# Reordering the first loads, transposes and cluster assignments of a routed-attention kernel, with one weight load and two lerps moved

## The chip, the cores and the metric

One core of one Trainium2 chip. The metric is device time in microseconds (us) of one execution. A few executions came out some per cent slower than the rest of the same kernel; they are called slow. All runs quoted as times are fast ones unless a sentence says otherwise. The time before was 252.65 us as the median of four executions (252.64 to 252.88; the three made first gave 252.67).

## The reference, cut to what matters

4 batches, 8 heads, 768 positions, 64 columns a head. Every query and key is assigned to the nearest of its head's 16 centroids; a query sees only the keys of its own cluster. The output goes through a channel mix with three matrix products.

```python
c_n = centroids / (np.linalg.norm(centroids, axis=-1, keepdims=True) + 1e-06)   # 8 x 16 x 64
q_assign = np.argmax(np.einsum('bhsd,hcd->bhsc', q_n, c_n), axis=-1)            # k_assign alike
mask = q_assign[:, :, :, None] == k_assign[:, :, None, :]
scores = scale * np.matmul(q, k.transpose(0, 1, 3, 2))
scores = np.where(mask, scores, -1000000000.0)
attn = softmax(scores) @ v                                   # shortened here
# x: the heads side by side, 4 x 768 x 512; x_prev: x one position earlier
xk = mu_k * x + (1.0 - mu_k) * x_prev
xr = mu_r * x + (1.0 - mu_r) * x_prev
k = np.maximum(xk @ w_k, 0.0)
v = k * k @ w_v
r = 1.0 / (1.0 + np.exp(-(xr @ w_r)))
return r * v
```

## The kernel before

The kernel walks through 192 score steps: 16 pairs of heads, 12 steps a pair. One step is a score product on TensorE (PE), an exponential on ScalarE (ACT) and, six steps later, the product with the values. The mask costs no pass of its own: each operand of the score product has 64 rows of data and 16 rows with the one-hot of its cluster.

```python
def scores(t):
    ...
    nc.tensor.matmul(st[:, 0:512], kc, a[rows, 0:512], start=True, stop=True)      # L286
    nc.tensor.matmul(st[:, 512:S], kc, a[rows, 512:S], start=True, stop=True)      # L287
    nc.scalar.activation(pt, st, AF.Exp, bias=-BIG, scale=BIG)                     # L289
```

The one-hot rows come in two ways. Pair 0 is done at the start in pieces: transposes of q and k (`first_trans`), products with the centroids (`first_aff`), one-hots transposed back and copied, half by VectorE (DVE) and half by ACT (`first_onehot`). From pair 1 on, one product `affps` is followed on DVE by a transpose, a maximum, a comparison and a transpose, and a DMA on SyncE's queue (SP) puts the rows `oht` into `aug`.

The order at the start, which the change alters, with cuts:

```python
nc.scalar.dma_start(cn_sb, centroids.rearrange("h c d -> (h c) d"))   # 32 KB
nc.scalar.preload_act_table(AF.Sqrt)
load_head(0, nc.sync, nc.scalar)          # q of pair 0 on SP's queue, k on ACT's, 192 KB each
...
use_pe(8)                                 # warm-up products on zeros
...                                       # norms of the centroids on DVE and ACT
nc.tensor.transpose(cnt_ps.rearrange("d h c -> d (h c)"), cn_sb, ident)
nc.vector.tensor_copy(cblk[0:64, :, 0, :], cnt_ps)
nc.vector.tensor_copy(cblk[64:128, :, 1, :], cnt_ps)
first_trans(0, 0)
first_trans(0, 1)
use_pe(4)
first_trans(1, 0)
first_aff(0, 0)
first_aff(0, 1)
first_trans(1, 1)
first_aff(1, 0)
...
first_onehot(0)
first_aff(1, 1)
```

What is put beside the steps. `forced` runs on PE within a step, `at` behind it:

```python
for i in range(4):
    at(7 + i // 2, load_wk, i)            # four pieces of w_k, GpSimd's queue
forced = {
    0: lambda: more(1, 0, 4, nc.vector, ps_o),    # transposes of pair 1
    1: lambda: more(1, 4, 4, nc.vector, ps_o),
    2: lambda: more(1, 8, 4, nc.vector, ps_o),
    3: lambda: first_onehot(1),
    4: lambda: aff_mm(1),
}
...
at((62, 66, 70, 74)[n] if n < NP else x + 4, sh2)   # the lerp into xr on DVE, L358
```

From step 58 on, slices of the channel mix (`psk`, `psr`, `psv`) are pushed in between. `psr` needs `xr`.

The softmax here doesn't subtract the row's maximum and nothing guards it: scores larger than these inputs give would overflow.

Of the kernel before, what the change touches and what calls it, by code (L numbers as in the profile page):

```python
# [16 lines left out]
def kernel(  # L17
# [13 lines left out]
    nc = tc.nc  # L31
# [4 lines left out]
    NP = H // 2  # L36
# [32 lines left out]
    ps_o = ctx.enter_context(tc.tile_pool(name="ps_o", bufs=2, space=bass.MemoryType.PSUM))  # L69
# [21 lines left out]
    def load_head(h, eng_q, eng_k):  # L91
        if h == 0:
            nat[0] = loadp.tile([128, 2, 2 * GW], F32, name="qk_rows", tag="qk_nat")
        for i, (src, eng) in enumerate(((q, eng_q), (k, eng_k))):
            eng.dma_start(
                nat[0][:, i, h * GW:(h + 1) * GW].rearrange("p (m e) -> p m e", e=2 * D),
                src[0, h].rearrange("(m p r) d -> p m (r d)", p=128, r=2))
# [128 lines left out]
    def first_trans(t, i):  # L226
        if t == 0 and i == 0:
            qkT[0] = qktp.tile([128, 4, GW], F32, name="qkT")
        g = 2 * i + t
        ps = ps_w.tile([128, GW], F32, name="trps0", tag="w") if t == 0 else \  # L230
            ps_o.tile([128, GW], F32, name="trps1", tag="out2")
        for c2 in range(NCH // 2):
            m = t * GW + c2 * 128
            nc.tensor.matmul(ps[:, c2 * 128:(c2 + 1) * 128], nat[0][:, i, m:m + 128], ident,
                             is_transpose=True, start=(c2 == 0), stop=(c2 == NCH // 2 - 1))
        if i == 0:
            nc.vector.tensor_copy(qkT[0][:, g, :], ps)
        else:
            nc.scalar.copy(qkT[0][:, g, :], ps)
        casts(0, g)  # L240

    def first_aff(t, i):
        if i == 0:
            first[t] = ps_w.tile([128, 2, NCH, C], F32, name="aff0", tag="w") if t == 0 else \
                ps_o.tile([128, 2, NCH, C], F32, name="aff1", tag="out2")
        ps = first[t]
        for c2 in range(NCH // 2):
            nc.tensor.matmul(ps[:, i, 2 * c2:2 * c2 + 2, :], qkT[0][:, 2 * i + t, c2 * 128:(c2 + 1) * 128],
                             cblk[:, t, :, :], start=True, stop=True)
        if i == 1:  # L250
            rmax = clup.tile([128, 2 * NCH], F32, name="rmax0")
            psv = ps.rearrange("p i c e -> p (i c) e")
            nc.vector.tensor_reduce(rmax, psv, axis=AX.X, op=ALU.max)
            oh = first[t] = clup.tile([128, 2 * NCH, C], BF16, name="oh0")
            nc.vector.tensor_tensor(oh, psv, rmax[:, :, None].to_broadcast([128, 2 * NCH, C]),
                                    op=ALU.is_ge)
# [187 lines left out]
    def at(t, fn, *args):  # L444
        todo.setdefault(t, []).append(lambda: fn(*args))

    with tc.manual_schedule():

        warm = constp.tile([128, 512], BF16)
        nc.vector.memset(warm, 0.0)  # L450
        nc.scalar.dma_start(cn_sb, centroids.rearrange("h c d -> (h c) d"))
        nc.scalar.preload_act_table(AF.Sqrt)
        load_head(0, nc.sync, nc.scalar)
        load_head(1, nc.sync, nc.scalar)
        load_rows(1, nc.sync, nc.scalar)
        load_v(0, nc.sync)
# [3 lines left out]
        def use_pe(m):  # L460
            wps = ps_st.tile([128, S], F32, name="wps", tag="st")
            for i in range(m):
                nc.tensor.matmul(wps[:, 0:512], warm[:, 0:128], warm, start=True, stop=True)  # L463
# [13 lines left out]
        cn_rnorm = constp.tile([H * C, 1], F32)  # L477
        nc.vector.reciprocal(cn_rnorm, cn_norm)
        nc.vector.tensor_scalar_mul(cn_sb, in0=cn_sb, scalar1=cn_rnorm)
        cnt_ps = ps_o.tile([D, H, C], F32, name="cnt_ps", tag="out2")  # L480
        nc.tensor.transpose(cnt_ps.rearrange("d h c -> d (h c)"), cn_sb, ident)
        nc.vector.tensor_copy(cblk[0:64, :, 0, :], cnt_ps)
        nc.vector.tensor_copy(cblk[64:128, :, 1, :], cnt_ps)
        first_trans(0, 0)
        first_trans(0, 1)
        use_pe(4)
        first_trans(1, 0)
        first_aff(0, 0)
        first_aff(0, 1)
        first_trans(1, 1)  # L490
        first_aff(1, 0)
        load_rows(2, nc.sync, nc.sync)
        load_v(1, nc.sync)
        vcast(0)
        for i in range(1, NX):
            init_ring(i)
        first_onehot(0)
        first_aff(1, 1)

        def more(n, i, m, eng=None, pool=None):  # L500
            for i in range(i, i + m):
                trans_pe(n, i, eng or nc.vector, pool)
# [24 lines left out]
        at(6, load_mu)  # L527
        at(31, less_one)
        for i in range(4):
            at(7 + i // 2, load_wk, i)  # L530
            at((29, 53, 55, 57)[i], load_wv, 2 * i)
            at((60, 62, 64, 66)[i], scale_wv, 2 * i)
        for i in range(2):
# [2 lines left out]
        W = 2 * NCH  # L536

        forced = {
            0: lambda: more(1, 0, 4, nc.vector, ps_o),
            1: lambda: more(1, 4, 4, nc.vector, ps_o),  # L540
            2: lambda: more(1, 8, 4, nc.vector, ps_o),
            3: lambda: first_onehot(1),
            4: lambda: aff_mm(1),
        }
        at(3, load_rows, 3, nc.sync, nc.sync)
# [2 lines left out]
        for n in range(NPAIR):  # L548
            s = n * W
            off = (6, 3, 2, 1)[n] if n < NP else 0  # L550
            if n + 4 < NPAIR:
                if n + 4 < NP + 2:
                    at(s + (16 if n == 0 else 9), load_rows, n + 4, nc.sync, nc.sync)
                elif n < NP:
                    for i in range(8):
                        at(s + (8 if n == 2 else 12) + i // 2, load_qk, n + 4, i // 4, i % 4)
                else:
                    for i in range(8):
                        at(s + (12 if n == NP else 9) + i, load_qk, n + 4, i // 4, i % 4)
            if n + 2 < NPAIR:  # L560
                if n < NP:
                    for i in range(6):
                        forced[s + i + off] = lambda n=n, i=i: more(n + 2, 2 * i, 2)
                    a = (13, 10, 9, 8)[n]
                    h = 1 if n == 0 else 2
                    for i in range(h):
                        forced[s + a + i] = lambda n=n, i=i, h=h: aff_mm(n + 2, i, h)
                    d = a + h - 5
                else:
                    if n == NP:  # L570
                        a = (9, 10, 11, 12, 15)
                    elif n == NP + 1:
                        a = (3, 4, 5, 6, 11)
                    elif n == NP + 2:
                        a = (1, 2, 3, 4, 9)
                    elif n == NP + 3:
                        a = (0, 1, 2, 3, 8)
                    else:
                        a = (-1, 0, 1, 2, 5)
                    for g in range(4):  # L580
                        at(s + a[g], trans, n + 2, g)
                    forced[s + a[4]] = lambda n=n: aff_mm(n + 2)
                    d = a[4] - 4
                at(s + 5 + d, aff_max, n + 2)
                at(s + 6 + d, aff_back, n + 2, [nc.sync])
                at(s + (3 if n == 0 else 8), load_v, n + 2, nc.sync)
            if n + 1 < NPAIR:
                at(s + 7, vcast, n + 1)
            at(s + W - 1, norm, 2 * n)
            e = s + W + NCH  # L590
            at(e - 1, norm, 2 * n + 1)
            if n == 0:
                at(e + 3, xtr, n)
            elif n < NP - 1:
                for i in range(3):
                    at(e + 3 + i, xtr, n, i, 3)
            elif n in (NP - 1, NPAIR - 1):
                x = e + (3 if n < NP else 2)
                at(x - 1, xtr, n)
            else:  # L600
                at(e, xt_dma, n)
                x = e + (4 if n % NP == NP - 1 else 6 if n == NPAIR - 2 else 14)

            def sh(n=n):
                b, j = divmod(n, NP)
                if j == 0:
                    mixes[b] = Mix(b)
                mixes[b].shift(n)

            def sh2(n=n):  # L610
                b, j = divmod(n, NP)
                mixes[b].shift_r(n)

            def enq(n=n):
                b = n // NP
                queue.extend(mixes[b].slices())
                rate[0] = len(queue) / (H * NCH + (b == 0)) if b < B - 2 else (len(queue) - HOLD) / (H * NCH - NCH - 4)
                credit[0] = 0.0
            at((33, 48, 50)[n] if n < NP - 1 else x, sh)
            at((62, 66, 70, 74)[n] if n < NP else x + 4, sh2)  # L620
            if n % NP == NP - 1:
                at(e + 4 if n < NP else x + 1, enq)

# [49 lines left out]
```

## Time and profile before

| | before |
|---|---|
| median, us | 252.65 |
| span of the profiled execution, us | 250.9 |
| PE busy / idle, us | 238.7 / 12.2 |
| first score (step 0) starts | 10.87 |
| step 5, the first score after the affinities of pair 1 | 15.57 |
| step 24, the first score of pair 2 | 32.33 |
| step 72, the first score of pair 6 | 75.01 |
| step 84 | 89.91 |
| last score (step 191) starts | 210.04 |

The prediction below shows the profile's lines themselves. From the timeline at the start of the kernel before (start, length, engine, line, operation, output<-input, in brackets the idle time before it and what ended that):

```profile
3.10 0.22 DVE L470 CUSTOM_DVE_ANT_0 cn_sq<-cn_sb 128x64 f32<-128x64 f32 x1 [1.70 <-DMA cn_sb<-in_centroids_dram]
...
11.39 3.11 ACT L289 ACTIVATE pt<-st 128x768 bf16<-128x768 f32 x4 [0.67 <-PE st L287]
```

The centroids are first used at 3.10 us. The first four exponentials take 3.11 us together: they run back to back.

### The profile page before, as it was taken

What the parts mean: (1) busy time and instruction counts of PE and PEld (TensorE: products, weight loads), DVE (VectorE), ACT (ScalarE), POOL (GpSimd) and SP (SyncE); (2) the same over time, 40 slices, a digit from 0 to 9 for tenths busy, and PEclk for the clock granted to TensorE, in tenths of its full rate; (3) what the DMA queues carried; (4) which work ended last, traced back from release to release, by engine and by line L of the source; (5) the groups of instructions that cost most, each with busy time, mean ns of one, the idle gap of its engine ahead of it and who ended that gap; (6) DMA issues with size and microseconds to landing.
All of it is one profiled execution on the core that took longest, in us unless ns stands there. A gap on an engine that the chain in (4) does not pass through costs nothing.

```text
span 250.9 us, 6203 instructions
## 1 busy us (share of the span) xinstructions
PE 238.7 (95%) x2364; PEld 146.5 (58%) x2395; DVE 176.6 (70%) x340; ACT 189.4 (75%) x271; POOL 106.0 (42%) x190
## 2 busy tenths in 40 slices
PE   8999989998998999999999999999999998899994
PEld 3866766765665555555676555556566555355442
DVE  3576778698899994979967778679844427865222
ACT  5398988999897977878999877878899785146210
POOL 2968848571999737080827153712801000000000
PEclk9999999999999999999999999999999999999999
DMA  6995897879978586965959689794121121110122
GB/s 176 260 258 94 153 280 143 112 140 168 178 114 170 92 176 127 201 123 120 206 67 157 80 185 131 167 163 152 34 79 29 47 70 48 56 72 0 70 98 86
DMA packets 102462, 31.87 MB, mean 127 GB/s; under 512 B 74721, under 2 KB 98977, under 8 KB 102433
## 3 DMA queue, kind: packets, MB, share of 16 engines
q1 hardware_dynamic: 98352, 27.97, 54.3%
q0 software_dynamic: 2208, 2.62, 7.0%
q10 hardware_dynamic: 1872, 0.89, 1.3%
q8 instruction: 19, 0.31, 0.5%
q14 instruction: 11, 0.08, 0.1%
HBM read 24.15 MB, written 6.29 MB: 121 GB/s over the span
## 4 chain that ended last, share of the span: by engine, by line
PE 75%; DVE 10%; ACT 8%; issue 2%; DMA 2%; SPq 0%; DVEq 0%; ACTq 0%
PE psv L405 15%; PE st L286 13%; PE out L299 10%; PE psk L382 10%; PE psr L394 7%; ACT pt L289 7%; PE st L287 6%; PE psk L373 5%; PE affps L194 4%; DMA aug<-oht 2%; PE wps L463 2%; DVE xr L358 2%; DVE k L388 1%; DVE oht L217 1%; DVE xk L358 1%
## 5 line engine op out<-in xcount | busy, mean ns | idle before, releaser
L289 ACT ACTIVATE pt<-st 128x768 bf16<-128x768 f32 x192 | 148.2, 811 | 23.2 <-PE st L287 22.8
L175 POOL TENSOR_SCALAR aug<-qkT 64x384 bf16<-64x384 f32 x128 | 74.8, 584 | 73.1 <-DVE qkT L145 52.2
L286 PE MATMUL st<-aug 80*128 80x512 bf16 x192 | 73.1, 381 | 2.5 <-ACT pt L289 1.0
L299 PEld LDWEIGHTS <-pt 128*128 128x128 bf16 x1152 | 59.9, 97 | 26.6 <-ACT pt L289 1.4
L299 PE MATMUL out<-vt,pt 128*128 128x65 bf16 x1152 | 66.0, 193 | 0.9 <-ACT pt L289 0.8
L287 PE MATMUL st<-aug 80*128 80x256 bf16 x192 | 51.9, 270 | 0.0
L405 PE MATMUL psv<-w_v_sb,k 128*128 128x512 bf16 x173 | 44.5, 378 | 1.4 <-ACT tanh L397 0.7
L387 ACT ACTIVATE kr<-psk 128x512 bf16<-128x512 f32 x48 | 28.8, 601 | 8.1 <-PE psk L382 5.6
L388 DVE TENSOR_TENSOR k<-kr 128x512 bf16<-128x512 bf16 x48 | 22.4, 473 | 17.0 <-ACT kr L387 16.9
L382 PE MATMUL psk<-xk,w_k_sb 128*128 128x512 bf16 x113 | 30.6, 378 | 1.5 <-DVE t L198 0.8
L412 DVE SCALAR_TENSOR_TENSOR out_sb<-tanh,psv 128x512 f32<-128x512 bf16 x23 | 15.7, 682 | 21.7 <-PE psv L405 17.8
L286 PEld LDWEIGHTS <-aug 80*128 80x128 bf16 x192 | 18.7, 97 | 17.3 <-issue 7.8
L397 ACT ACTIVATE tanh<-psr 128x512 bf16<-128x512 f32 x24 | 14.4, 599 | 19.1 <-PE psr L394 18.5
L405 PEld LDWEIGHTS <-k 128*128 128x128 bf16 x184 | 16.1, 97 | 16.4 <-issue 2.4
L287 PEld LDWEIGHTS <-aug 80*128 80x128 bf16 x192 | 18.9, 98 | 9.7 <-issue 1.6
L394 PE MATMUL psr<-w_r_sb,xr 128*128 128x512 bf16 x91 | 23.7, 378 | 0.2
L145 DVE STREAM_TRANSPOSE qkT<-qk_nat 128x384 f32<-128x384 f32 x40 | 21.5, 557 | 0.0
L182 POOL CAST vt<-v_nat 128x384 bf16<-128x384 f32 x32 | 17.0, 560 | 9.5 <-DMA v_nat<-in_v_dram 8.7
L312 DVE TENSOR_TENSOR xn<-out,rs 128x384 bf16<-128x384 f32 x32 | 17.8, 558 | 1.1
L198 DVE STREAM_TRANSPOSE t<-affps 128x384 f32<-128x384 f32 x15 | 8.7, 580 | 14.0 <-PE affps L194 13.9
L382 PEld LDWEIGHTS <-w_k_sb 128*128 128x128 bf16 x128 | 11.2, 97 | 10.2 <-issue 0.9
L358 DVE SCALAR_TENSOR_TENSOR xk<-diff,mu_k_sb,xt 128x768 bf16<-128x768 bf16 x16 | 16.7, 1043 | 0.6
(65 smaller groups left out, 206.2 us busy)
## 6 DMA issues: line engine op xcount, KB each, us to landing
v_nat<-in_v_dram SPq DMA_DIRECT2D x16, 384.0 KB, 4.2
out_dram<-out_sb SPq DMA_DIRECT2D x23, 256.0 KB, 2.8
qk_nat<-in_q_dram SPq DMA_DIRECT2D x40, 96.0 KB, 4.3
qk_nat<-in_k_dram SPq DMA_DIRECT2D x40, 96.0 KB, 3.6
qk_rows<-in_q_dram SPq DMA_DIRECT2D x5, 384.0 KB, 4.4
qk_rows<-in_k_dram SPq DMA_DIRECT2D x4, 384.0 KB, 5.3
aug<-oht SPq DMA_DIRECT2D x60, 24.0 KB, 2.0
w_k_sb<-in_moe_w_k_dram POOLq DMA_DIRECT2D x4, 256.0 KB, 5.6
```

Source lines behind the costliest of these rows:

```text
L145: nc.vector.transpose(qkT[n][:, g, :], nat[n][:, g // 2, (g % 2) * GW:(g % 2 + 1) * GW])
L175: nc.gpsimd.tensor_scalar(augv(n, g)[0:64, par, :], in0=qkT[n][64 * par:64 * par + 64, g, :], scalar1=qk_scale, scalar2=1.0, op0=ALU.mult, ...
L286: nc.tensor.matmul(st[:, 0:512], kc, a[rows, 0:512], start=True, stop=True)
L287: nc.tensor.matmul(st[:, 512:S], kc, a[rows, 512:S], start=True, stop=True)
L289: nc.scalar.activation(pt, st, AF.Exp, bias=-BIG, scale=BIG)
L299: nc.tensor.matmul(o[:, (qc + NCH // 2) % NCH, :], pts[bh * NCH + c][:, qc * 128:(qc + 1) * 128], vts[n % NR][:, tt, 2 * (c % 3) + c // 3, ...
L358: nc.vector.scalar_tensor_tensor(out=d, in0=diff, scalar=mu[:, j:j + 1], in1=cur, op0=ALU.mult, op1=ALU.add)
L382: nc.tensor.matmul(ps, w_k_sb[:, j, ii * 128:(ii + 1) * 128], self.xk[:, j, 0:512], start=(j == 0), stop=(j == NJ - 1))
L387: nc.scalar.activation(kr, src, AF.Relu)
L388: nc.vector.tensor_tensor(dst, kr, kr, op=ALU.mult)
L394: nc.tensor.matmul(ps, self.xr[:, j, sl], w_r_sb[:, j, :], start=(j == 0), stop=(j == NJ - 1))
L405: nc.tensor.matmul(self.psvt, self.k2[:, i, sl], w_v_sb[:, i, :], start=(i == 0), stop=(i == NI - 1))
```

## The change

The intent: q and k of the first heads, the large loads, should not stand behind the small one; PE should transpose them instead of waiting for the centroids; and head 1's clusters, wanted only at step 6, should not delay head 0's first score. One w_k load moves out of the way of the cluster rows of pair 2, and two lerps move behind an affinity transpose that PE awaits. I name the five parts A to E.

```diff
+        load_head(0, nc.sync, nc.scalar)                                    # A
         nc.scalar.dma_start(cn_sb, centroids.rearrange("h c d -> (h c) d"))
         nc.scalar.preload_act_table(AF.Sqrt)
-        load_head(0, nc.sync, nc.scalar)
 ...
+        first_trans(0, 0)                                                   # B
+        first_trans(0, 1)
         cnt_ps = ps_o.tile([D, H, C], F32, name="cnt_ps", tag="out2")
 ...
-        first_trans(0, 0)
-        first_trans(0, 1)
         use_pe(4)
-        first_trans(1, 0)                                                   # C
         first_aff(0, 0)
         first_aff(0, 1)
+        first_trans(1, 0)
         first_trans(1, 1)
-        first_aff(1, 0)
 ...
         first_onehot(0)
-        first_aff(1, 1)
+        first_aff(1, 0)
 ...
-            at(7 + i // 2, load_wk, i)
+            at((7, 7, 8, 27)[i], load_wk, i)                                # D
 ...
-            0: lambda: more(1, 0, 4, nc.vector, ps_o),
-            1: lambda: more(1, 4, 4, nc.vector, ps_o),
-            2: lambda: more(1, 8, 4, nc.vector, ps_o),
-            3: lambda: first_onehot(1),
+            0: lambda: first_aff(1, 1),                                     # C
+            1: lambda: more(1, 0, 4, nc.vector, ps_o),
+            2: lambda: more(1, 4, 4, nc.vector, ps_o),
+            3: lambda: (more(1, 8, 4, nc.vector, ps_o), first_onehot(1)),
 ...
-            at((62, 66, 70, 74)[n] if n < NP else x + 4, sh2)
+            at((62, 66, 72, 75)[n] if n < NP else x + 4, sh2)               # E
```

## The prediction

> **What bounds the kernel now.** I read the page first. One core, span 250.9 us, TensorE at full granted clock and busy 95%:
>
> ```profile
> span 250.9 us, 6203 instructions
> ...
> PE 238.7 (95%) x2364; PEld 146.5 (58%) x2395; DVE 176.6 (70%) x340; ACT 189.4 (75%) x271; POOL 106.0 (42%) x190
> ```
>
> So all idle time of PE is 250.9 - 238.7 = 12.2 us, and a change of order alone, with the same work, can only win or lose there. The table of stretches says where that idle time is (columns: stretch, its length, then busy us of each engine, clock, DMA share, GB/s):
>
> ```profile
> 0.00:11.00 11.00, 9.62 (x62) 6.69 (x63) 4.57 (x15) 4.52 (x6) 5.81 (x19) 1.00 0.74 203
> 11.00:21.50 10.50, 9.86 (x105) 6.75 (x104) 7.81 (x13) 9.94 (x13) 7.73 (x20) 1.00 0.77 210
> 21.50:33.00 11.50, 10.77 (x147) 7.37 (x148) 8.16 (x17) 9.26 (x13) 10.29 (x21) 1.00 0.84 161
> 33.00:50.00 17.00, 16.48 (x230) 12.04 (x228) 12.88 (x25) 16.04 (x22) 10.14 (x19) 1.00 0.91 174
> ...
> 70.00:79.00 9.00, 8.10 (x81) 4.95 (x82) 8.93 (x16) 7.26 (x12) 8.25 (x11) 1.00 0.75 126
> ...
> 90.00:215.00 125.00, 122.49 (x1248) 73.86 (x1269) 90.77 (x178) 102.76 (x148) 42.54 (x72) 1.00 0.61 116
> ```
>
> Three regimes. Until about 60 us the exponentials pace the kernel (9.94 of 10.50 us of ACT busy in the second line, 16.04 of 17.00 in the fourth). From 70 to 79 us DVE is full, 8.93 of 9.00, and PE loses 0.90. After 90 us PE is full. A delay or gain of the ramp that survives to 60 us is carried to the end one for one, because from there a fixed amount of PE work follows. Busy PE in the first 11 us proves nothing: 12 of its matmuls are warm-ups on zeros.
>
> Next the chain of waits, in order of time (start, length, what), for the point that limits the ramp:
>
> ```profile
> 25.55 0.99 DVE oht L217
> ...
> 26.56 0.51 SPq L219
> 27.07 0.04 issue
> 27.12 5.12 DMA aug<-oht
> 32.24 0.09 issue
> 32.33 0.38 PE st L286
> ```
>
> Step 24, the first scores of pair 2, waits for the 24 KB cluster rows, 5.12 us under way. The waits of PE give that stop as 0.7 us, and the later one as 0.8 us:
>
> ```profile
> PE st L286 <- DMA aug<-oht: 0.7, 1, 0.7
> ```
>
> ```profile
> PE psk L382 <- DVE t L198: 0.8, 1, 0.8
> ```
>
> Last the timeline at the start, which the change reorders:
>
> ```profile
> 3.59 1.28 ACT L475 ACT_TABLE_LOAD   x1
> ...
> 3.99 0.25 DVE L479 TENSOR_SCALAR cn_sb<-cn_sb,cn_rnorm 128x64 f32<-128x64 f32 x1
> ...
> 4.79 0.94 PE L234 MATMUL trps<-ident,qk_rows 128*128 128x128 f32 x6
> 5.04 0.28 DVE L482 COPY cblk<-cnt_ps 64x128 f32<-64x128 f32 x1 [0.79 <-PE cnt_ps L481]
> ...
> 6.76 1.42 PE L248 MATMUL aff<-cblk,qkT 128*128 128x32 f32 x12
> ...
> 9.94 0.79 ACT L271 COPY aug<-ohps 16x768 bf16<-16x768 bf16 x1 [0.88 <-PE ohps L264]
> ```
>
> Centroids are ready at 4.24, affinities run from 6.76 to 8.18, the one-hots end with ACT's copy at 10.73, the first score starts at 10.87.
>
> **What the Trainium skill says.** (1) DMA: Bandwidth & Descriptors, "Queues, rings and completion order": each SDMA engine round-robins between the queue rows that have work, packet by packet, and takes the descriptors of one ring in order. The trace agrees: the pair-1 cluster rows issued at 18.90 landed in 1.9 us; the same 24 KB at 26.56, behind two tiny loads on the SP queue and beside w_k on POOL's, took 5.4. (2) The same page, "Specifications": below 512 B a transfer is not at line rate. The two mu loads of 2 KB took 5.7 and 9.7 us. (3) ScalarE: Activation LUTs, "What ACT_TABLE_LOAD costs": about 1283 ns a load; the trace has 1.28 us. (4) TensorE: Matmul & The Clock Gate, Part 1: until activity opens the gate the array runs at half clock. Agreed: the first warm-ups come every 0.43 us, the later ones every 0.22 (1.03 us for four, with the last one's drain). So transposes put earlier can't start before the eight warm-ups end at about 4.58.
>
> **The change part by part.** No arithmetic is added or taken away; five things move.
>
> *k before the centroids.* k of head 0 is now issued at 0.74 with q, the centroids at about 1.23 behind it. Landings before: centroids 0.74 + 2.3 = 3.0, q 3.6, k 1.23 + 3.8 = 5.0. Estimate from these: q and k together by 4.2, centroids 4.2 to 4.5. The chain behind them stays: 3.10 (first use) to 4.24 is 1.14 us, so they are normalized at about 5.5. The q copy (0.56) now stands before the two cblk copies (0.57 together), so cblk is ready at about 5.5 + 1.13 + 0.05 = 6.7. On PE the affinities no longer have three transposes ahead of them: 6.76 - 0.33 + what the new order costs cold, about 6.6. The later of the two rules: 6.7 against 6.76. The table load for Exp slides to about 4.9 to 6.1 and the k copy behind it to 6.6, still in time for the second half of the affinities. First score: 10.87, within -0.1 and +0.3. Gain nothing.
>
> *Head 1's second affinities behind step 0.* Before, they ran from 9.83 to 10.68, in the shadow of ACT's copy, which ends at 10.73: they were free. Now six matmuls (0.73) stand between scores 0 and 1 in place of four transposes (0.44): score 1 is 0.29 later, and ACT, which ran exponentials 0 to 3 back to back, idles 0.27.
>
> *The pair-1 transposes one step later, the last four together with the one-hots in step 3.* In step 3 the one-hots start 0.44 behind the four transposes, with the 0.27 above: ACT's one-hot copy goes from 14.53 to about 15.1, exponential 4 from 15.34 to 15.9. DVE must copy the last transpose (0.69) before its own one-hot copy, which goes from 14.12 to about 15.1. The pair-1 affinities need the buffer that this copy frees: 14.78 becomes 15.75, score 5 from 15.57 to 16.5, and the cluster chain (transpose, max, one-hot, transpose, DMA) shifts whole. Its second transfer landed just before score 12 at 21.48, so score 12 goes to about 22.4: +0.95 us.
>
> *w_k, one piece of four from step 8 to 27.* The pieces issued at 20.66 to 23.41 land 3.9 to 8.1 us later, the last at 31.5, in front of the landing that step 24 waits for. Pieces 3 and 4 land 29.3 and 31.5: each costs 1.4 to 2.2 us there (estimate). Without the fourth the wait moves from 32.24 to about 30.5, and with the chain's shift of 0.95 to about 31.5. Alone this would be worth the whole 0.7 us of PE idle: score 24 at 31.6. With the ramp 0.95 late PE gets there at 32.55. So 32.33 becomes 32.55: +0.2. The moved piece falls at about 37.5 to 40.5, where DMA is quiet at 38 to 40 us, and the queue wants it only at 61 us.
>
> *Two xr lerps from steps 70 and 74 to 72 and 75.* The lerp (1.25 us) at 76.07 stood before the affinity transpose at 77.25 whose buffer PE awaited; now it stands behind it, and the transpose runs at 76.1. PE's 0.79 us stop goes. DVE gets no shorter, and xr is wanted at 84.9, with the last lerp at about 84 in the new order: I count 0.65 of the 0.79.
>
> Sum: first score 0, step 24 +0.2, step 73 -0.65: -0.45 us. 252.67 - 0.45 = 252.2.
>
> **Rivals.** A: the centroids land at once behind k (4.0) or the copies overlap better, and the one-hot delay is half of mine; then scores 12 to 24 are 0.4 late, PE reaches step 24 at 32.0, and the whole is 32.0 - 32.33 - 0.75 = -1.1: 251.6. For it: DMA took centroids in 2.3 us when first. Against: both queues share the same 16 engines, and k goes first in the same ring. B: the centroids land at 4.9 instead, all of the start shifts 0.5, and score 24 goes to 33.0; with the lerp gain it ends at 252.7. For it: k's own 3.8 us. C: the DVE stop only moves. DVE is full from 63 to 95 us, so PE waits for xr, or for the eviction of the first output tile, instead; the -0.65 shrinks to -0.2: 252.7. D: the moved w_k piece now delays pair 3's rows, which land at 41.0 for step 36 at 41.98: 1 us of slack holds nearly all of its 1.4 us of transfer. At worst +0.5.
>
> **Range and chances.** Single terms are unsure by: start -0.1 to +0.4, one-hots and chain 0.4 to 1.3, lerps -0.2 to -0.8. Together 251.4 to 253.0 eight times in ten, centre 252.2. Two per cent are 5 us; the changed places hold less than that in idle PE, and no mechanism here adds it. Faster 0.01, same 0.98, slower 0.01.
>
> **What would show it.** First score near 10.9; ACT no longer back to back between exponentials 0 and 3; affinities of pair 1 near 15.7; score 12 near 22.4; at step 24 no DMA wait and PE near 32.5; one w_k load alone near 37.5; the 0.8 us stop before psk near 77 gone, with the same PE busy time. Wrong if: the first score starts before 10.5 or after 11.4; score 12 comes before 21.9; step 24 still waits for the cluster rows; or a new stop of PE over 0.4 us stands between 77 and 92 us.

## The result, and the profile after

The changed kernel took 254.06 us (median of four, 253.66 to 254.59) against 252.65 before. The ratio is 1.0055, 95% interval 1.0035 to 1.0074. Ratios here are the mean time of one kernel's fast runs over that of the other's of the same rounds, so not quite the ratio of the medians. It is slower, by less than 2%, and above the predicted range of 251.4 to 253.0. The profiled execution was the fastest of the four, 253.66.

The page of the changed kernel:

```profile
span 251.8 us, 6204 instructions
...
PE 239.0 (95%) x2364; PEld 146.4 (58%) x2395; DVE 175.1 (70%) x340; ACT 189.6 (75%) x271; POOL 105.4 (42%) x190
```

PE is busy for 239.0 us, 0.3 more than before; the span grew by 0.9. So 0.6 us of the loss is idle time of PE, and the stretches tell where (columns as in the prediction):

```profile
0.00:11.00 11.00, 9.27 (x53) 5.74 (x53) 4.04 (x14) 4.00 (x6) 4.31 (x16) 1.00 0.72 185
11.00:21.50 10.50, 9.66 (x97) 6.77 (x97) 6.73 (x12) 8.77 (x12) 7.63 (x20) 1.00 0.80 223
21.50:33.00 11.50, 11.23 (x158) 7.92 (x156) 8.01 (x14) 10.43 (x15) 10.14 (x21) 1.00 0.60 102
...
70.00:79.00 9.00, 7.73 (x88) 5.12 (x88) 7.70 (x15) 7.18 (x13) 8.18 (x11) 1.00 0.89 121
```

In the second stretch ACT, which paces it, has 8.77 us of work where it had 9.94. The third stretch is better than before: PE 11.23 against 10.77. From 70 to 79 us PE is worse, 7.73 against 8.10, and DVE is no longer full.

The start of the changed kernel, from its timeline:

```profile
5.25 0.23 DVE L470 CUSTOM_DVE_ANT_0 cn_sq<-cn_sb 128x64 f32<-128x64 f32 x1 [3.85 <-DMA cn_sb<-in_centroids_dram]
...
7.51 1.50 PE L248 MATMUL aff<-cblk,qkT 128*128 128x32 f32 x12
...
11.66 0.38 PE L286 MATMUL st<-aug 80*128 80x512 bf16 x1 [0.19 <-ACT aug L271]
...
12.19 3.29 ACT L289 ACTIVATE pt<-st 128x768 bf16<-128x768 f32 x4 [0.67 <-PE st L287]
...
15.87 0.79 ACT L271 COPY aug<-ohps 16x768 bf16<-16x768 bf16 x1 [0.40 <-PE ohps L264]
...
16.71 0.85 PE L194 MATMUL affps<-qkT,cblk 128*32 128x384 f32 x8 [0.45 <-ACT aug L271]
```

The centroids are first used at 5.25 us, 2.15 later than before; the affinities start at 7.51 instead of 6.76, and the first score at 11.66 instead of 10.87. Then a second delay is added: ACT stands idle 0.40 us before its one-hot copy, and PE 0.45 us behind that copy, before the affinities of pair 1.

The DMA issues of the first 1.3 us, changed kernel (output<-input, queue, kind, count, KB each, median us from issue to landing):

```profile
qk_rows<-in_q_dram SPq DMA_DIRECT2D x2, 192.0 KB, 3.8
qk_rows<-in_k_dram ACTq DMA_DIRECT2D x1, 192.0 KB, 3.7
cn_sb<-in_centroids_dram ACTq DMA_DIRECT2D x1, 32.0 KB, 4.0
```

Before, the line of the centroids was:

```profile
cn_sb<-in_centroids_dram ACTq DMA_DIRECT2D x1, 32.0 KB, 2.3
```

The same 32 KB take 4.0 us behind k and 2.3 us ahead of it. They are also issued half a microsecond later (1.25 against 0.74).

Last, the waits of PE (what waits, what for, us in total, times, longest), and the chain of waits near the new stop at step 72 (start, length, what):

```profile
PE st L286 <- DMA aug<-oht: 1.5, 2, 1.2
```

```profile
74.64 0.38 SPq L219
75.02 0.04 issue
75.06 1.89 DMA aug<-oht
76.95 0.09 issue
77.05 0.38 PE st L286
```

The wait for cluster rows at step 24 is gone, but PE waits 1.2 us for the rows of pair 6 at step 72 (the other wait in that line is 0.28 us at step 48). DVE had these rows ready at 72.08, but SP was then issuing two loads of k, and the rows came behind them:

```profile
71.59 2.79 SPq L81 DMA_DIRECT2D qk_nat<-in_k_dram  x2
74.48 2.43 SPq L219 DMA_DIRECT2D aug<-oht  x4
```

The second of the four, the last that step 72 needs, was issued at 75.06 and landed at 76.95. In the kernel before, the rows were ready at 71.62 and the first was issued at 71.65.

How much later each score step starts than in the trace of before, in us, worked out as the difference of the start times of its first score product. One trace for each kernel; e1 to e10 are the experiments below, e11 is the changed kernel once more:

| step | changed | e11 again | e1 A | e2 all but A | e3 D | e4 all but D | e5 C | e6 E | e8 mu | e9 B | e10 mu+B |
|---|---|---|---|---|---|---|---|---|---|---|---|
| 0 | +0.79 | +0.85 | +1.87 | -0.02 | +1.05 | +0.83 | -0.78 | +0.24 | -0.14 | +0.20 | -0.29 |
| 5 | +1.93 | +1.99 | +1.87 | +1.12 | +1.06 | +1.97 | +0.36 | +0.24 | -0.14 | +0.20 | -0.29 |
| 23 | +1.68 | +1.77 | +1.55 | +0.87 | +0.76 | +2.39 | +0.05 | 0.00 | -0.42 | +0.15 | -0.56 |
| 24 | +0.89 | +0.97 | +1.35 | +0.07 | -0.04 | +1.60 | -0.23 | -0.12 | -1.22 | -0.25 | -1.35 |
| 71 | +0.76 | +1.32 | +1.42 | +0.10 | +0.18 | +1.46 | -0.07 | +0.04 | -1.05 | -0.08 | -1.07 |
| 72 | +2.04 | +1.32 | +1.96 | +0.10 | +0.54 | +1.46 | -0.07 | +0.30 | -1.05 | -0.08 | -0.88 |
| 74 | +1.07 | +0.37 | +1.41 | -0.85 | +0.17 | +0.51 | -0.07 | -0.67 | -1.06 | -0.08 | -1.06 |
| 84 | +1.08 | +1.39 | +1.41 | +0.16 | +0.17 | +1.52 | -0.07 | +0.10 | -1.06 | -0.07 | -1.06 |
| 191 | +0.86 | +1.59 | +1.48 | +0.72 | +0.30 | +1.64 | -0.34 | +0.24 | -1.31 | -0.35 | -1.28 |

### The profile page after: what moved, and what is told of

It is laid out like the page before. It is cut to its first block, busy times and chain, and to the rows that moved or that the text cites. A ratio compares the mean times of both kernels' runs of the same rounds, so it can differ in the third digit from the quotient of the medians.

```text
span 251.8 us, 6204 instructions
## 1 busy us (share of the span) xinstructions
PE 239.0 (95%) x2364; PEld 146.4 (58%) x2395; DVE 175.1 (70%) x340; ACT 189.6 (75%) x271; POOL 105.4 (42%) x190
## 2 busy tenths in 40 slices
DMA packets 102461, 31.87 MB, mean 127 GB/s; under 512 B 74720, under 2 KB 98976, under 8 KB 102432
## 4 chain that ended last, share of the span: by engine, by line
PE 70%; DVE 12%; ACT 6%; SPq 4%; issue 3%; DMA 3%; DVEq 0%; ACTq 0%
PE psv L405 14%; PE st L286 13%; PE out L299 9%; PE psk L382 8%; PE psr L394 7%; PE st L287 6%; PE psk L373 5%; ACT pt L289 4%; SPq L81 4%; PE affps L194 3%; DVE xr L358 3%; DVE qkT L145 2%; PE trps L161 2%; DMA cn_sb<-in_centroids_dram 2%; DMA aug<-oht 2%
## 5 line engine op out<-in xcount | busy, mean ns | idle before, releaser
L175 POOL TENSOR_SCALAR aug<-qkT 64x384 bf16<-64x384 f32 x128 | 73.1, 571 | 71.2 <-DVE qkT L145 48.7
L358 DVE SCALAR_TENSOR_TENSOR xr<-diff,mu_r_sb,xt 128x768 bf16<-128x768 bf16 x16 | 16.6, 1039 | 0.0
```

Source lines behind the costliest of these rows:

```text
L175: nc.gpsimd.tensor_scalar(augv(n, g)[0:64, par, :], in0=qkT[n][64 * par:64 * par + 64, g, :], scalar1=qk_scale, scalar2=1.0, op0=ALU.mult, ...
L358: nc.vector.scalar_tensor_tensor(out=d, in0=diff, scalar=mu[:, j:j + 1], in1=cur, op0=ALU.mult, op1=ALU.add)
```

## The experiments

The theory T: A delays the centroids and with them the first score; C delays the clusters of pair 1 by about 1.1 us more; D wins back what it can at step 24; E gains at step 74. The rivals are numbered R1 to R8, and each expectation says what T and the rival expect of that run. They were in three batches: e1 to e4, e5 to e8 and e9 to e11, each batch on one chip with its own runs of the kernel before (medians 252.51, 252.34 and 252.55). All results were correct.

**e1, part A alone.** The old order on PE, k's load ahead of the centroids.

```diff
+        load_head(0, nc.sync, nc.scalar)
         nc.scalar.dma_start(cn_sb, centroids.rearrange("h c d -> (h c) d"))
         nc.scalar.preload_act_table(AF.Sqrt)
-        load_head(0, nc.sync, nc.scalar)
```

> The kernel before, with k of head 0 loaded ahead of the centroids and nothing else. Theory T (late centroids): they land near 5.2 us instead of 3.1, and in the old PE order all transposes stand behind them, so the first score goes from 10.87 to about 12.7 (+1.9); by step 24 the DMA wait there takes 0.7 of it back (+1.2); time about 253.9. Rival R1 (the order of the loads is harmless, the late first score comes from the order on TensorE): first score within 0.2 of 10.87 and time within 0.3 of before.

Measured: two runs of four were fast, 254.18 and 254.1; two were slow, 260.43 and 263.95. Ratio of the fast ones 1.0070 [1.0042, 1.0097]. The centroids took 4.1 us and were first used at 5.38; the first score came 1.87 us late. PE's waits have a line that the kernel before doesn't have:

```profile
PE cnt_ps L481 <- DVE cn_sb L479: 1.9, 1, 1.9
```

What follows: A delays the centroids by itself, and in the old order the whole delay falls on PE. The new order on PE (B, and from C the three transposes put behind the affinities) softens it: the affinities start 7.51 - 5.25 = 2.26 us after the centroids' first use in the changed kernel, and 8.63 - 5.38 = 3.25 us here. That order buys 1.0 us, but only because A made the centroids late. The two slow runs have no trace; what they did is open.

**e2, all but part A.** The changed kernel with the centroids first again.

```diff
         nc.vector.memset(warm, 0.0)
-        load_head(0, nc.sync, nc.scalar)
         nc.scalar.dma_start(cn_sb, centroids.rearrange("h c d -> (h c) d"))
         nc.scalar.preload_act_table(AF.Sqrt)
+        load_head(0, nc.sync, nc.scalar)
```

> The changed kernel with the centroids first in the queue again, all other parts kept. T: first score near 10.7, score 5 near 16.6 (1.0 later than before, from the moved clusters), score 24 near 32.4; the wait for the cluster rows at step 72 stays, about 1 us, since it comes from the moved w_k piece; time about 252.9. Rival R2 (the wait at step 72 comes from the late ramp, not from w_k): no DMA wait at step 72 and about 251.9.

Measured: 253.26 us (252.46 to 253.86), 1.0030 [0.9997, 1.0063]. The centroids took 2.3 us again. The first score is 0.02 us early, and the shift is 0.81 to 0.82 us smaller than in the changed kernel from step 0 to step 24. What follows: A costs 0.8 us at the start. TensorE's clock opened at 5.5 us in this trace and at 6.5 in the changed kernel's, but e4, which has A and where it opened at 5.3, is 0.83 late as well, so the opening is not the reason. In time the two ratios differ by 0.0025, some 0.6 us; their intervals overlap, so the size is the traces'. The clusters still come 1.12 + 0.02 = 1.14 us late by step 5. The stop at step 72, which T expected, did not come.

**e3, part D alone.**

```diff
-            at(7 + i // 2, load_wk, i)
+            at((7, 7, 8, 27)[i], load_wk, i)
```

> The kernel before, with the fourth w_k piece moved to step 27 and nothing else. T: score 24 at 31.6 instead of 32.33, but all loads after 38 us land later, and the cluster rows of pair 6 (landed 0.5 us before step 72 in the kernel before) come after it: a wait of about 1.5 us at step 72, which lets the vector engine catch up, so its 0.8 us stop in step 73 goes; time 252.4 to 252.9. R2: no wait at step 72, the 0.7 us are kept; about 251.9.

Measured: 252.84 us, but from 251.34 to 254.99; 1.0025 [0.9967, 1.0082]: not conclusive in time. In the trace the first score was 1.05 us late, though nothing ahead of step 7 had been changed. The cause is in the warm-up products. First the line of e3, then that of before, both from the timeline of PE:

```profile
6.07 1.58 PE L463 MATMUL wps<-warm 128*128 128x512 bf16 x4
```

```profile
5.57 1.03 PE L463 MATMUL wps<-warm 128*128 128x512 bf16 x4
```

The same four products of the same operands take 1.58 us instead of 1.03: TensorE's clock opened later in this execution. So a single trace of the start is a draw, and only differences that several traces repeat can be given to a change. What follows for D: the shift falls from 0.76 at step 23 to -0.04 at step 24. The wait for the cluster rows there is gone, and PE sets the pace. But PE then waits 0.5 us at step 48 and 0.3 at step 72 for cluster rows. A stop of 0.3 to 0.5 us at step 48 stands in three of the five traces with D (changed, e2, e3) and in none of the eight without; by step 60 it is made up.

**e4, all but part D.**

```diff
-            at((7, 7, 8, 27)[i], load_wk, i)
+            at(7 + i // 2, load_wk, i)
```

> The changed kernel with the fourth w_k piece back at step 8. T: the wait for cluster rows at step 24 is back (score 24 near 33.9), none at steps 48 and 72; time about 253.4, and less scatter than the changed kernel. R2: the wait at step 72 stays, and the one at step 24 is added: about 254.7.

Measured: 254.52 us (254.21 to 255.15), 1.0088 [1.0064, 1.0112]. Step 24 starts at 33.92, as T said, but by luck: the 0.9 us that PE waits for cluster rows stand at step 12, not at step 24. From the timeline of PE:

```profile
23.88 0.38 PE L286 MATMUL st<-aug 80*128 80x512 bf16 x1 [0.93 <-DMA aug<-oht]
```

These are the rows of pair 1, landed at 23.79. In front of them in SP's queue stood a load of v, which landed at 23.47 here and at 22.05 in the changed kernel. The piece of w_k that e4 moves back was issued only at 25.13, so D can't be the cause. At step 24 the rows of pair 2 landed at 33.74, 1.87 us later than in the changed kernel, but PE, late since step 12, needed them no sooner.

What follows: the shift of 1.60 at step 24, against 0.89 in the changed kernel, doesn't measure D. A better comparison is e1, which is as late at step 12 (+1.56 against +1.69) and has no D; there step 24 does wait:

```profile
33.68 0.38 PE L286 MATMUL st<-aug 80*128 80x512 bf16 x1 [0.53 <-DMA aug<-oht]
```

Its shift at step 24 is 1.35 against 0.89. So D is worth about half a microsecond within the change, an estimate from these traces. The times point the same way, 1.0088 against 1.0055 and 1.0060 for the two measurements of the changed kernel, but the intervals overlap. And there is no stop at step 72. Kernels with D (changed, e3) and without D (e1, e6) have shown it, and others of both sorts haven't.

**e5, part C alone** (the `first_trans`, `first_aff` and `forced` lines marked C above; loads, order on PE before them, w_k and lerps as before).

```diff
-        first_trans(1, 0)
         first_aff(0, 0)
         first_aff(0, 1)
+        first_trans(1, 0)
         first_trans(1, 1)
-        first_aff(1, 0)
...
-            3: lambda: first_onehot(1),
+            3: lambda: (more(1, 8, 4, nc.vector, ps_o), first_onehot(1)),
```

> The kernel before, with only head 1's transposes and affinities moved behind head 0's (the second half behind the first score, pair 1's transposes one step later). Theory T: the first score stays at 10.9, score 5 comes 1.0 to 1.2 later, score 24 about 0.8 to 1.1 later, and that is carried to the end: 253.4 to 253.7. Rival R3 (the shift is slack that the wait at step 24 swallows): score 24 within 0.2 of 32.33 and about 252.6.

Measured, five rounds: 253.42 us (252.43 to 254.27) against 252.34; 1.0043 [1.0018, 1.0069]. Between steps 0 and 5 the shift grows by 0.36 + 0.78 = 1.14 us, as in the changed kernel and in e2. The profiled execution was the fastest of the six, and its first score 0.78 us early, so that its step 24 came no later than before. The times say otherwise: 1.08 us between the medians. What follows: C by itself makes the kernel slower, by about what it delays the clusters of pair 1. That its cost reaches the end was measured in time, not seen in a trace.

**e6, part E alone.**

```diff
-            at((62, 66, 70, 74)[n] if n < NP else x + 4, sh2)
+            at((62, 66, 72, 75)[n] if n < NP else x + 4, sh2)
```

> The kernel before, with only the two xr lerps moved from steps 70 and 74 to 72 and 75. T (the stop only moves): score 74 about 0.85 earlier than before, but by score 84 all of it is given back at a wait for xr; time within 0.3 of before, about 252.6. Rival R5 (my prediction): 0.65 of it is kept, about 252.0.

Measured: 252.85 us (252.4 to 253.22), 1.0020 [0.9998, 1.0042]. The shift goes from +0.30 at step 72 to -0.67 at step 74, and is +0.10 at step 84. What follows: PE's stop before `psk` goes, as intended, and what is won is lost again within ten steps. e11 below shows where.

**e7, the changed kernel with the centroids on GpSimd's queue,** so that they stand behind nothing in their queue.

```diff
-        nc.scalar.dma_start(cn_sb, centroids.rearrange("h c d -> (h c) d"))
+        nc.gpsimd.dma_start(cn_sb, centroids.rearrange("h c d -> (h c) d"))
```

> The changed kernel, with the centroids' load issued by GpSimd on a queue of its own at the start and k still first on ScalarE's queue. T (it is the place behind k in one ring that makes them late): they land by 4.2, the first score is within 0.2 of 10.87, and the time is that of the changed kernel less about 0.8, near 253.2. Rival R4 (q and k hold the shared engines, whatever queue the centroids are on): they land at 4.8 or later, first score at 11.4 or later, near 254.

Measured: 258.12 us (254.02 to 261.11). Four of six runs were slow, the profiled one (259.09) among them; the two fast ones give 1.0102 [1.0057, 1.0147]. The DMA issues of this slow execution:

```profile
cn_sb<-in_centroids_dram POOLq DMA_DIRECT2D x1, 32.0 KB, 4.9
```

The centroids land at 6.17 us, later than behind k (5.23). T had put the delay down to the place behind k in one queue; with a queue of their own they should have come early. That part of T fell. The rival, that the load shares the engines with 192 KB of q and 192 KB of k already under way, is nearer, but no run loads the centroids on GpSimd's queue with nothing else under way, so a slow start of that queue is not excluded and this isn't settled either. In the slow execution the clock opened at 20.6 us only: the wide score products took 0.61 us until then, and 0.39 after 22 us.

**e8, another remedy for step 24: the kernel before with the two `mu` loads moved** from SP's queue, where they stood in front of the cluster rows of pair 2, to GpSimd's, three steps later.

```diff
-            nc.sync.dma_start(mu_k_sb, moe_mu_k.rearrange("(j p) -> p j", p=128))
-            nc.sync.dma_start(mu_r_sb, moe_mu_r.rearrange("(j p) -> p j", p=128))
+            nc.gpsimd.dma_start(mu_k_sb, moe_mu_k.rearrange("(j p) -> p j", p=128))
+            nc.gpsimd.dma_start(mu_r_sb, moe_mu_r.rearrange("(j p) -> p j", p=128))
...
-        at(6, load_mu)
+        at(9, load_mu)
```

> The kernel before, with the two tiny mu loads taken off the sync queue (where they stand in front of pair 2's cluster rows) and issued by GpSimd behind the w_k pieces. T: pair 2's rows no longer wait behind them in the ring, land at least 1 us before 32.24, score 24 at 31.6 to 31.8; about 252.0. Rival R6 (the rows are held by w_k on the shared engines, not by mu in their ring): landing and score 24 within 0.3 of before, 252.5.

Measured: 251.7 us (251.09 to 251.9), 0.9973 [0.9951, 0.9994]: faster than before, by 0.7 us. The DMA issues about that time, first of e8, then of the kernel before:

```profile
aug<-oht SPq DMA_DIRECT2D x4, 24.0 KB, 3.8
```

```profile
aug<-oht SPq DMA_DIRECT2D x4, 24.0 KB, 4.9
```

The rows come in 3.8 us instead of 4.9, and are there at 30.76 instead of 32.24. Step 24 starts 1.22 us earlier, of which 0.80 is won between steps 23 and 24. What follows: taking the two loads of 2 KB, in pieces of 4 bytes, out of the way won as much between steps 23 and 24 as moving the 256 KB piece of w_k did in e3 (0.80 us each), and no later wait for cluster rows shows in the trace. The edit does two things, another queue and three steps later, and the last piece of w_k also landed sooner (28.76 against 31.48); which of these freed the rows isn't separated.

**e9, part B alone.**

```diff
+        first_trans(0, 0)
+        first_trans(0, 1)
         cnt_ps = ps_o.tile([D, H, C], F32, name="cnt_ps", tag="out2")
 ...
-        first_trans(0, 0)
-        first_trans(0, 1)
```

> The kernel before, with only the first head's transposes put ahead of the centroids' on TensorE and on VectorE; the loads stay in the old order. Theory T: the only part of the start that can help, worth 0.1 to 0.3 us at the first score (10.6 to 10.8 when the clock gate opens near 5.0 us), swallowed in part by the wait at step 24: 252.2 to 252.6 where before is 252.5. Rival R7 (the q copy now in front of the two cblk copies on VectorE costs what is won): first score within 0.1 of the kernel before at the same opening of the gate, or later.

Measured: 252.38 us (251.7 to 253.84) against 252.55; 0.9998 [0.9969, 1.0028]. What follows: with the centroids early, B is worth nothing that can be measured.

**e10, e8 and part B together,** the edits of e8 and e9.

> Mu loads on GpSimd's queue and the first head's transposes first, both on the kernel before. T: no wait at step 24, so the earlier start is kept too: 0.7 + 0.2 below before, near 251.6. R7: no more than the mu loads alone, 0.7 below before, 251.8.

Measured: 251.34 us (250.56 to 251.76), 0.9945 [0.9925, 0.9966]. It beats both kernels: 1.4 us under the one before by the ratio. Step 0 is 0.15 us earlier than in e8, where the clock opened at nearly the same time (4.4 and 4.5 us). Whether B adds anything to e8 in time is not shown: the two ran on different chips.

**e11, the changed kernel once more,** unaltered.

> The changed kernel once more, unaltered, on the chip of the other runs. T (late centroids +0.7, clusters +1.0, w_k -0.8, lerps 0 to +0.5): ratio to before 1.004 to 1.006, first score 11.5 to 11.8 whatever the opening of the clock gate below 6.4 us. Rival R8 (the first measurement fell on an unlucky opening of the clock gate and the change is neutral): ratio within 0.002 of 1.

Measured: 254.13 us (253.91 to 254.42), 1.0060 [1.0042, 1.0079]. The first result holds. This trace has the same delays at the start (0.85 at step 0, 1.14 more by step 5) but no stop at step 72: that stop is not part of the change. And it shows E plainly: the shift goes from 1.32 to 0.37 at step 74 and is 1.39 at step 84. From the timeline of PE in this trace, and then of DVE:

```profile
85.27 0.81 PE L394 MATMUL psr<-w_r_sb,xr 128*128 128x512 bf16 x3
...
86.50 0.39 PE L394 MATMUL psr<-w_r_sb,xr 128*128 128x512 bf16 x1 [0.42 <-DVE xr L358]
```

```profile
85.19 1.25 DVE L358 SCALAR_TENSOR_TENSOR xr<-diff,mu_r_sb,xt 128x768 bf16<-128x768 bf16 x1
```

The first `psr` has three of its four products done and stands 0.42 us before the fourth: the last lerp, one step later in the program, ends only at 86.44. In the kernel before, the four ran together at 84.90 with no stop.

## Why the prediction was wrong

It said 252.2 us, the measurement said 254.06. It added up 0 at the first score, +0.2 at step 24 and -0.65 at step 73.

1. **The centroids: the step that failed first, and most.** "Estimate from these: q and k together by 4.2, centroids 4.2 to 4.5", and from that "First score: 10.87, within -0.1 and +0.3". The mechanism was right, and nearly the length of the path behind it: first use plus 1.14 + 1.13 + 0.05 = 2.32 us gives 5.25 + 2.32 = 7.57 for the affinities, against 7.51 measured. (In part by luck: `cblk` was ready at 7.36 already, and the four warm-up products that follow the centroids' transpose held PE until about 7.5.) The term that was mis-sized is the landing: 5.23 in the changed kernel, 5.27 in e4, 5.29 in e11. The estimate read the 32 KB as if they only had to follow k by their size; they took 4.0 us from issue, longer than k's own 192 KB (3.7). The first score was 0.79 late, and e2 takes exactly that back. Rival B named it, with 4.9 for the landing and 0.5 for the shift.
2. **The clusters of head 1 and pair 1.** Predicted +0.95 by score 5 and 12, measured 1.14 between scores 0 and 5 in the changed kernel, e2, e4, e5 and e11 alike. The order of things was as told: the exponentials 0 to 3 take 3.29 us instead of 3.11 and are no longer back to back. One link was wrong: the prediction let the affinities of pair 1 wait for DVE's one-hot copy; they started at 16.71, when ACT's had ended at 16.66 and DVE's at 16.39. A part came back: PE's idle time before step 12 fell from 0.51 to 0.27 us, and the 0.90 left there (1.69 - 0.79) is close to the prediction.
3. **Step 24.** "At step 24 no DMA wait" was right: the rows land at 31.87, and the step starts by PE's own pace at 33.21. The prediction had +0.2 here from a punctual first score. Putting in what was measured, 0.2 + 0.79 (centroids) + 0.19 (clusters) - 0.24 (step 12) = 0.94; the trace has 0.89. D is what brought the rows in time: the second of them was 2.8 to 3.1 us under way in the five traces with D, and 4.3 to 5.1 in the six that have neither D nor the moved `mu` loads.
4. **The lerps.** "I count 0.65 of the 0.79" failed outright: the gain between steps 71 and 74 was 0.7 to 0.95, larger than counted, and by step 84 nothing of it was left, in four traces (e2, e4, e6, e11). The prediction had written the reason down as rival C: DVE is full (30.7 us of the 32 from 63 to 95 us, before as in e11), so a lerp moved behind one reader stands in front of the next. In the changed kernel's first trace the same stretch reads differently, since the stop at step 72 came first, and it ends alike: +0.76 at step 71, +1.08 at step 84.
5. **The stop at step 72** was in no part of the prediction. The rows of pair 6 had 0.47 us of slack in the kernel before (landed at 74.54, used at 75.01), which I did not look at. It came in the traces of the changed kernel, e1, e3, e6 and e7, and not in the eight others. Neither of the two accounts, the moved w_k or the late ramp (the late start of the steps), fits that list. What does fit it is the time that SP took to issue the rows: from ready on DVE to the issue of the second, the last that step 72 needs, 1.65 to 2.98 us in those five traces and 0.58 to 0.87 in the eight others. In the changed kernel and e7 the loads of k in front took most of it, in e1, e3 and e6 the rows' own first issue (1.5 to 1.6 us instead of 0.5 to 0.8). Why an issue takes that long in one execution and not in the next stays open. By step 84 the stop left about 0.3 us in the first trace and nothing in e1 and e3, where PE's stop before `psk` shrank from 0.8 to 0.3 and 0.4 us.

Together, in the first trace: 0.89 at step 24, +0.19 up to step 84, -0.22 behind it, is 0.86 at the last score, for a span 0.9 us longer. The other three runs were 0.4 to 0.9 us slower than the profiled one and have no trace; e11, traced at 254.28, has 1.59 at the last score. Behind step 84, where no line was changed, the traces drift between -0.28 (e9) and +0.56 us (e2) against the one before, so a difference of that size at the last score says nothing of a part.

The range failed in a way of its own. Rivals B and C both came true, each was written with 252.7, and they were weighed as alternatives; added, B's +0.5 and C's +0.45 make 252.2 + 0.95 = 253.15, outside the range that was given. The chance of 0.98 for "within 2%" was right.

## What to carry to other kernels

A small load that everything waits for goes first: 32 KB put behind 192 KB were first used 2.15 us later, while k landed 0.5 us earlier and q 0.5 us later. Before moving work off an engine that is full, look for the next reader of that work, for there the gain is given back; and before a wait is attacked by shifting a large load, look at what stands in the same queue in front of it, since in single traces moving two 2 KB loads won as much at step 24 as moving 256 KB. Trust a difference at the start of a kernel only when several traces repeat it.

## What the Trainium skill lacked or had wrong

- TensorE: Matmul & The Clock Gate, Part 1, says that the opening of the clock varies from run to run and that the ramp is under 1% of a typical span, so not worth fitting. The variation agrees: the clock records of the traces open at 5.0 us before, 4.2 in e5, 7.2 in e3 and 6.5 in the changed kernel. But with identical code ahead of it the first score came 0.14 us early (e8) and 1.05 late (e3), and in e5, which differs there by the order of a few small products, 0.78 early; that is about as large as any part of this change. In e7's slow execution it opened at 20.6 us, and that execution took 259.09 us against 254.02 for the fastest of the kernel, 2% more. The page has no warning that this limits what one trace of a start can tell. The two kernels with slow runs, e1 and e7, are those whose PE waited longest for the centroids (1.9 and 1.3 us); whether that is why is not shown. The column of the granted clock in the stretches reads 1.00 throughout and does not show it.
- DMA: Bandwidth & Descriptors, "Anatomy of one DMA", gives a fixed 2.0 us plus the size over 436 GB/s for one DMA of GpSimd's queue, by estimate some 2.1 us for 32 KB. e7, with q and k under way, took 4.9 us; on ACT's queue the same load took 2.3 us first and 4.0 behind k. No page says how to size a small load among large ones.
- The same page has nothing on what a load in 4-byte pieces does to the loads queued behind it. Behind two such loads of 2 KB the 24 KB cluster rows of the same queue took 4.9 us; with the two on another queue and issued three steps later they took 3.8 (e8). Which of the two counted, no run separates.
